# Seven block products of a mixture of experts: y tiles joined on another engine and at another time, and bank-opening products on another operand

## The chip, the cores and the metric

One core of one Trainium2 chip. The metric is the device time of one execution in microseconds; lower is better. The times below are those of single executions, and the profile is that of one further execution.

## The reference

A gated attention gives the input of a mixture of experts with 16 experts in 4 groups. Cut to what is computed:

```python
# attention: B, S, D = 8, 1856, 256; d_qk = 64
scores = (1.0 / S) * np.matmul(z, z.transpose(0, 2, 1))
attn = np.maximum(scores, 0.0) ** 2
x = (u * np.matmul(attn, v)).reshape(B * S, D)          # 14848 rows of 256
# experts: G = Eg = 4, F = 1024
g_logits = x @ w_group
g_idx = np.argmax(g_logits, axis=1)                     # g_w: its softmax weight
e_logits = xg @ w_expert[g]                             # rows xg of group g
e_idx = np.argmax(e_logits, axis=1)                     # e_w: its softmax weight
h = np.maximum(xg[mask_e] @ w1[g, e], 0.0)
ye = h @ w2[g, e]
out[tok_idx] = (g_w * e_w)[:, None] * ye
```

Each row of x goes to one expert; its result is scaled by one number and written to the row that it came from.

## The kernel before, in words

**Stages.** The attention part takes about the first half of the time. It routes its rows as it goes: a row, with its weight and its number, is scattered to a bucket of its expert in DRAM. Then come the experts, sorted by how many rows they hold: the first four (NOLD = 4) in 12 blocks of up to 512 rows, the other 12 (numbers 4 to 15) each as a pair of halves of equal width (512 rows each for expert 4, 424 for expert 14). All matmuls are done in parts: an operand is split into a high and a low part, and a product is low x high, high x high and high x low.

**A block (experts 0 to 3).** `phase1` (L784) is the first product and the relu: 8 slices f of 128 hidden rows with 6 matmuls each, evicted by ACT (L797) and DVE (L803). `phase2_t` (L848) is the second product, transposed: for each of two halves d of the 256 outputs, 24 matmuls (8 slices f, 3 parts q) into one bank. ACT copies the bank out as 16-bit halves (L872, L877); SP then issues one transposing DMA for each tile t of 128 rows (L882), from `yp` to `yr`. What brings a tile to its end is `finish(t, m)` (L886): a **join** of the halves into a tile y (L888, DVE), the **scale** by the row's weight (L894 on DVE for a block, L896 on ACT for a pair), and the **scatter** to the output (L897, issued by POOL). `phase2_t` does not run `finish`; it returns one such function for each tile, and the caller keeps them in the list `unsent` and pops them where it chooses.

**A pair (experts 4 to 15).** The first product of both halves together is done by seven block products in place of eight (`duo_phase1`, L1256): w1 and x are combined beforehand (`split_w1`, L1173, 8 steps; `split_duo`, L1223, 12 steps; both on DVE and ACT), and for each of four g there are products m = 1 to 7 of three matmuls each (L1274). They add up in PSUM banks that are never opened anew: ACT copies product 1 to bank Y (L1288) and product 5 to SBUF (L1291), DVE adds (L1293, L1297), ACT and DVE evict (L1282, L1283). The order of the 28 products is the list `seq` (L1304). In it, product 6 of a g adds onto the copy that L1288 has made. Then `phase2_t` runs for half 0 and for half 1. POOL splits w2 in eight steps (`split_w2`, L1191; L1197 and L1198), into w2 tiles that the second product reads; w2 comes by the tiles r0 and r1, into which the next expert's w1 is loaded when the splits are done.

**Order.** Program order is the order in which a scheduler is told of the instructions; it gives each engine a fixed order of its own, from the dependences and its own estimates. Instructions under `pin` keep their order among each other on their engine; in the pair stage, all of TensorE's instructions keep program order. So the places at which `finish` and the other small steps are called matter for DVE, ACT and POOL. In a pair they are these:
- The loop over `prods` (L1383) interleaves the products with the steps of `split_w2`, with the overflow planner (`planned`, L1386, at every fourth product) and with four pops of `unsent` (L1388, at lengths 12, 9, 6 and 3).
- In half 0, `slots` (L1405) holds the last product and steps of `split_w1` and `split_duo` (`chore`); a slot (d, k) is ahead of matmul k of half d of the outputs.
- In half 1, `slots` holds further such steps, four pops of `unsent` at (0, 3), (0, 9), (0, 15) and (0, 21) (L1433), and from (1, 10) on the first four products of the next expert (`lead`).

So half 0's four tiles are finished in half 1 and half 1's four in the next expert's first product: 92 tiles in all in `phase2_t` of the pairs. The last half (L1442) is done in another way, by `phase2`, which pops what is left in its first tile.

**The planner** (`plan`, L1043) works out an overflow path with some 47 small DVE steps; eleven of them work on 1024 elements. In the blocks it is advanced at L1327, from block 5 on, at every second f.

**Buffers.** Tiles of one tag share a number of buffers; a tile gets one when an earlier tile of that tag has had its last access. `y` has 3, `tm` has 2 (used in the pairs by `phase2` alone), `meta` (weights and row numbers of a half) has 4, and `at` has 3: w1's high part of a block expert, and later the tiles a, s and t of `split_w1` (L1180, L1182, L1188). In the hand-over to the pairs, `duo_banks` (L1248) opens the four banks y0, y1, z0 and z1 with one matmul each (L1254); its operand is `wt["h"][0]`, the high part of w1 of expert 3.

Of the kernel before, what the change touches and what calls it, by code (L numbers as in the profile page):

```python
# [9 lines left out]
F32 = mybir.dt.float32  # L10
F32R = mybir.dt.float32r
BF16 = mybir.dt.bfloat16
I32 = mybir.dt.int32
# [6 lines left out]
P = 128  # L20
# [9 lines left out]
def tile_glu_attn_moe(  # L30
# [715 lines left out]
    NOUT = sum((n + P - 1) // P for n in [bk[2] for bk in blocks] + [n for d in duos.values() for n in d])  # L746
    oviews = dram_disjoint_views(out, NOUT)
    ocnt = [0]
    rows_b = {}
    wts = {}  # L750

# [2 lines left out]
    def load_x(name, r0, n):  # L754

        xp = new_pl(f"xp_{name}").rearrange("p (g q) -> p g q", g=4)
        nc.sync.dma_start_transpose(xp[:, :, 0:n], bucket16[ds(r0, n), 0:2 * D])
        meta = sb("meta", [P, 4, 2], I32, 4, f"meta_{name}")
        nt = (n + P - 1) // P
        nc.sync.dma_start(  # L760
            meta[:, 0:nt, :], bucket[ds(r0, nt * P), D:D + 2].rearrange("(t p) w -> p t w", p=P)
        )
        return xp, meta
# [84 lines left out]
    def phase2_t(name, wt, hs, meta, n, outs, between, po=None, slots=(), order=range(NF)):  # L848
        po = po or [bank(ps_o, "o", f"yT_{name}_{d}") for d in range(ND)]
        order = list(order)  # L850
        yp = sb("ut", [P, ND, 512], F32, 2, f"yp_{name}").rearrange("p c q -> p (c q)").bitcast(U16)
        yr = new_rows(f"yr_{name}")
        tiles = [(t, min(P, n - t * P)) for t in range((n + P - 1) // P)]
        full, part = n // P, n % P

        yg = yp.rearrange("p (t g q) -> p t g q", g=4, q=P)
        if part:
            nc.gpsimd.memset(yg[:, full, :, part:P], 0)
        for d in range(ND):
            between(d)  # L860
            o = po[d][:, 0:n]
            prods = [(f, q) for f in order for q in range(3)]
            if d == 0:
                prods.sort(key=lambda x: x[1] == 2)
            for at, (f, q) in enumerate(prods):
                for fn in slots and slots.pop((d, at), ()):
                    fn()
                w0 = (f % 2) * 512 + (D if q == 0 else 0) + d * P
                nc.tensor.matmul(o, wt["2"][f // 2][:, w0:w0 + P], hs[f][q // 2][:, 0:n],  # L869
                                 start=(at == 0), stop=(at == 3 * NF - 1))  # L870
            if full:
                nc.scalar.copy(  # L872
                    out=yg[:, 0:full, 2 * d:2 * d + 2, :],
                    in_=o[:, 0:full * P].bitcast(U16).rearrange("p (t q h) -> p t h q", q=P, h=2),
                )
            if part:
                nc.scalar.copy(  # L877
                    out=yg[:, full, 2 * d:2 * d + 2, 0:part],
                    in_=o[:, full * P:n].bitcast(U16).rearrange("p (q h) -> p h q", h=2),
                )  # L880
        for t, m in tiles:
            nc.sync.dma_start_transpose(  # L882
                yr[:, t, 0:D].bitcast(U16).rearrange("p (g d) -> p g d", d=P),
                yg[:, t].rearrange("p g q -> p (g q)"),
            )
        def finish(t, m):  # L886
            y = sb("y", [P, D], F32, 3, f"y_{name}_{t}")
            pin(nc.vector.tensor_copy(  # L888
                out=y[0:m].bitcast(U16).rearrange("p (d q h) -> p d h q", d=ND, h=2),
                in_=yr[0:m, t, 0:D].bitcast(U16).rearrange("p (d h q) -> p d h q", d=ND, h=2),  # L890
            ))
            cw = meta[0:m, t, 0:1].bitcast(F32)
            if isinstance(name, int):
                nc.vector.tensor_scalar(out=y[0:m], in0=y[0:m], scalar1=cw, scalar2=None, op0=ALU.mult)  # L894
            else:
                nc.scalar.activation(out=y[0:m], in_=y[0:m], func=AF.Copy, scale=cw)  # L896
            nc.gpsimd.indirect_dma_start(  # L897
                out=outs(),
                out_offset=bass.IndirectOffsetOnAxis(ap=meta[0:m, t, 1:2], axis=0),
                in_=y[0:m],  # L900
                in_offset=None,
                bounds_check=N - 1,
                oob_is_err=False,
            )

        return [lambda t=t, m=m: finish(t, m) for t, m in tiles]
# [295 lines left out]
    def duo_rows(e):  # L1202
        n1, n2 = duos[e]
        r0 = regs(e)[1]
        lst = []
        at = 0
        while at < 2 * n1:
            n = min(512, 2 * n1 - at)
            xp = new_pl(f"xp_w{e}_{at}").rearrange("p (g q) -> p g q", g=4)
            nc.sync.dma_start_transpose(xp[:, :, 0:n], bucket16[ds(r0 + at, n), 0:2 * D])  # L1210
            lst.append((at, n, xp))
            at += n
        metas = []
        for h, n in enumerate((n1, n2)):
            meta = sb("meta", [P, 4, 2], I32, 4, f"meta_w{e}_{h}")
            nt = (n + P - 1) // P
            nc.sync.dma_start(
                meta[:, 0:nt, :], bucket[ds(r0 + h * n1, nt * P), D:D + 2].rearrange("(t p) w -> p t w", p=P)
            )
            metas.append(meta)  # L1220
        duo_x[e] = (lst, metas)
# [23 lines left out]

    banks = {}

    def duo_banks(wt):  # L1248
        for k in ("x0", "w", "p0"):
            banks[k] = bank(ps_s, "s", f"duo_{k}")  # L1250
        banks["p1"] = bank(ps_m, "m", "duo_p1")
        for k in ("y0", "y1", "z0", "z1"):
            banks[k] = bank(ps_o, "o", f"duo_{k}")
            nc.tensor.matmul(banks[k], wt["h"][0][:, 0:P], wt["h"][0][:, 0:512], start=True, stop=True)  # L1254

    def duo_phase1(e):  # L1256
        w = duos[e][0]
# [54 lines left out]
    for i, (e, r0, n) in enumerate(blocks):  # L1312
# [10 lines left out]
        def mid(f):  # L1323
            if i < NEARLY:
                early(i)
            elif i > 2 * NEARLY and f % 2 == 0:
                next(planned, None)  # L1327
            if i + 1 == NB and f > 3 and unsent:
                unsent.pop(0)()
# [42 lines left out]

        unsent = phase2_t(i, wts[e], hs, rows_b.pop(i)[1], n, next_view, mid2) or unsent

    duo_banks(wts[NOLD - 1])
    pe_order = ExitStack()
    pe_order.enter_context(tc.manual_schedule(engines={mybir.EngineType.PE}))
    wt = {"2": [wst[f"w{k}"] for k in range(4)]}
# [1 line left out]
    for e in range(NOLD, NE):  # L1380
        more = e + 1 < NE
        build2 = split_w2()
        while len(prods) > 1:  # L1383
            next(build2, None)
            if len(prods) % 4 == 0:
                next(planned, None)  # L1386
            if unsent and len(prods) < 14 and len(prods) % 3 == 0:
                unsent.pop(0)()  # L1388
            if more and len(prods) == 8:
                duo_w1(e + 1)  # L1390
                duo_rows(e + 1)
# [10 lines left out]
        def chore(n):  # L1402
            return lambda: [next(work, None) for _ in range(n)] if more else None

        slots = {(0, 4): [prods[0]]}  # L1405
        for d in range(ND):
            for k in range(0 if d else 6, 24, 3):
                slots.setdefault((d, k), []).append(chore(1))
# [5 lines left out]
        if more:  # L1414
# [15 lines left out]
            slots[(1, 10)] = slots.get((1, 10), []) + [ahead_products]  # L1430
            for k in (12, 14, 18, 20):
                slots.setdefault((1, k), []).append(lead(k))
            for k in (3, 9, 15, 21):  # L1433
                slots.setdefault((0, k), []).append(lambda: unsent.pop(0)() if unsent else None)
            unsent += phase2_t(f"w{e}_1", wt, hs[1], duo_x[e][1][1], n2, next_view, lambda d: None, po, slots)
            hs, prods = nxt["hs"], nxt["prods"]
        else:
# [75 lines left out]
```

## Time and profile before

| | us |
|---|---|
| median of 3 runs | 1468.46 |
| lowest and highest of them | 1468.35, 1470.37 |
| the profiled execution | 1471.43 |
| its span, first to last instruction | 1469.6 |
| TensorE matmuls busy (share) | 1428.8 (97%) |
| VectorE (DVE) busy | 1231.9 (84%) |
| ScalarE (ACT) busy | 1020.1 (69%) |
| GpSimd (POOL) busy | 394.0 (27%) |

The mean granted clock of TensorE is 0.989 of full speed. How to read the rows: PE is TensorE, SP issues DMAs. Matmuls are pipelined, so that one starts before the one ahead of it has ended; the distance of their starts is what one takes, and their "busy" time is modelled. "idle before <- X" is the time for which an engine did nothing ahead of an instruction, and what ended it. L12 is line 12 of the kernel before. Times are microseconds from the start of the span, if nothing else is said.

### The profile page before, as it was taken

Reading aid. Unit: us, or ns where it says so; the run is one execution under the profiler, and the core shown is the slowest. Engines: PE = TensorE matmul, PEld = TensorE weight load, DVE = VectorE, ACT = ScalarE, POOL = GpSimd, SP = SyncE. Lnnn points to the kernel's source line nnn. Section 1 sums busy time; section 2 is a strip of 40 time slices with the busy share of each in tenths; the row PEclk is TensorE's granted clock in tenths of the full one; section 3 lists DMA queues with packets and bytes.
Section 4 is the critical chain, followed back from the end, with each engine's and each line's share of the span. In section 5 each row is a group of like instructions: output and inputs, shape, how many; then the busy total and the mean of one; then the engine's idle time right before and its main releaser. Section 6 shows DMA issues by size and latency. Waiting matters only on the chain.

```text
span 1469.6 us, 22695 instructions
## 1 busy us (share of the span) xinstructions
PE 1428.8 (97%) x6981; PEld 1229.3 (84%) x6981; DVE 1231.9 (84%) x2460; ACT 1020.1 (69%) x1824; POOL 394.0 (27%) x462
## 2 busy tenths in 40 slices
PE   9999999999999999999999999979999999999986
PEld 7898888888888878888788989957788888888885
DVE  7889999989989899999986585977888888787873
ACT  8887887878877788777774444445666666666653
POOL 0002112220122202222205212333333444443433
PEclk9999999999999999999999999989999999999999
DMA  9998969889799887997884555514454454454531
GB/s 319 327 238 226 242 169 267 206 233 222 181 256 217 221 221 185 254 225 193 202 212 103 149 120 113 122 54 107 128 131 125 121 132 122 121 135 118 133 88 46
DMA packets 400045, 256.48 MB, mean 175 GB/s; under 512 B 244131, under 2 KB 355262, under 8 KB 399920
## 3 DMA queue, kind: packets, MB, share of 16 engines
q1 hardware_dynamic: 387984, 223.97, 61.6%
q0 software_dynamic: 11856, 30.90, 7.1%
q8 instruction: 55, 0.90, 0.3%
q14 instruction: 70, 0.57, 0.1%
q10 hardware_dynamic: 80, 0.13, 0.0%
HBM read 108.29 MB, written 89.21 MB: 134 GB/s over the span
## 4 chain that ended last, share of the span: by engine, by line
PE 78%; DVE 10%; issue 5%; DMA 2%; POOL 2%; ACT 2%; SPq 0%; DVEq 0%; ACTq 0%; POOLq 0%
PE o L403 13%; PE o L404 13%; PE o L406 12%; PE duo_p L869 11%; PE yT L869 5%; PE duo_y L1274 4%; PE sc L366 4%; PE sc L367 4%; PE ph L792 2%; PE duo_x L1274 2%; PE ph L793 2%; PE ph L794 2%; PE duo_w L1274 2%; PE duo_p L1274 1%; PE duo_z L1274 1%
## 5 line engine op out<-in xcount | busy, mean ns | idle before, releaser
L403 PE MATMUL o<-ah,vl 128*128 128x512 f32 (+2 forms) x960 | 354.5, 370 | 0.6 <-DVE ah L378 0.4
L404 PE MATMUL o<-ah,vh 128*128 128x512 f32 (+2 forms) x960 | 354.3, 369 | 0.0
L406 PE MATMUL o<-al,vh 128*128 128x512 f32 (+2 forms) x896 | 329.2, 370 | 0.0
L638 POOL DMA_INDIRECT bucket<-rows,di x121 | 137.9, 1140 | 376.4 <-issue 219.1
L370 ACT ACTIVATE r<-sc 128x512 f32<-128x512 f32 (+2 forms) x312 | 178.2, 571 | 66.5 <-PE sc L367 41.1
L403 PEld LDWEIGHTS o<-ah,vl 128*128 128x128 f32 x960 | 180.2, 188 | 30.5 <-DVE ah L378 0.8
L404 PEld LDWEIGHTS o<-ah,vh 128*128 128x128 f32 x960 | 180.2, 188 | 29.0
L381 DVE TENSOR_TENSOR al<-r,ah 128x512 fp32r<-128x512 f32 (+2 forms) x280 | 187.8, 671 | 17.3 <-PE pk L603 0.5
L406 PEld LDWEIGHTS o<-al,vh 128*128 128x128 f32 x896 | 167.9, 188 | 26.9 <-DVE al L381 0.7
L869 PE MATMUL duo_p<-hh_w,duo_w 128*128 128x496 f32 (+9 forms) x692 | 183.9, 379 | 4.0 <-POOL duo_w L1198 3.6
L377 ACT ACTIVATE r<-r 128x512 f32<-128x512 f32 (+2 forms) x284 | 174.2, 613 | 9.0
L869 PEld LDWEIGHTS duo_p<-hh_w,duo_w 128*128 128x128 f32 x692 | 131.6, 191 | 22.4 <-POOL duo_w L1198 4.2
L378 DVE CAST ah<-r 128x512 fp32r<-128x512 f32 (+2 forms) x284 | 117.4, 413 | 25.1 <-ACT r L377 20.3
L897 POOL DMA_INDIRECT out_dram<-y_w,meta_w x92 | 94.2, 1023 | 141.6 <-ACT y_w L896 123.0
L366 PE MATMUL sc<-zm,z2h 128*128 128x512 f32 (+2 forms) x312 | 120.3, 386 | 0.1
L367 PE MATMUL sc<-zm,z2l 128*128 128x512 f32 (+2 forms) x312 | 118.9, 381 | 0.0
L869 PE MATMUL duo_p<-hl_w,duo_w 128*128 128x496 f32 (+9 forms) x346 | 106.5, 379 | 0.0
L306 DVE STREAM_TRANSPOSE mt<-r 128x512 f32<-128x512 f32 x147 | 103.7, 705 | 0.6
L356 DVE TENSOR_TENSOR al<-at,ah 128x512 fp32r<-128x512 f32 (+1 forms) x168 | 94.9, 578 | 3.3 <-ACT ah L355 2.8
L355 ACT CAST ah<-at 128x512 fp32r<-128x512 f32 (+1 forms) x168 | 86.2, 532 | 9.1 <-DMA at<-sym 3.7
L869 PE MATMUL yT<-hh,w_e 128*128 128x512 f32 (+6 forms) x384 | 82.9, 334 | 0.0
L897 POOL DMA_INDIRECT out_dram<-y,meta x37 | 40.9, 1105 | 130.8 <-DVE y L894 124.9
(238 smaller groups left out, 2869.1 us busy)
## 6 DMA issues: line engine op xcount, KB each, us to landing
sym<-mt SPq DMA_DIRECT2D x126, 256.0 KB
duo_r<-in_w_dram SPq DMA_DIRECT2D x48, 512.0 KB
at<-sym SPq DMA_DIRECT2D x84, 256.0 KB
bucket<-padrow SPq DMA_DIRECT2D x32, 660.0 KB
at<-sym SPq DMA_DIRECT2D x84, 160.0 KB
vr<-in_v_dram SPq DMA_DIRECT2D x23, 512.0 KB
ut<-in_uT_dram SPq DMA_DIRECT2D x23, 512.0 KB
raw_e<-in_w_dram SPq DMA_DIRECT2D x16, 512.0 KB
```

Source lines behind the costliest of these rows:

```text
L366: held(nc.tensor.matmul(ps[:, 0:w], z2h[:, ks], zm, start=True, stop=False))
L367: held(nc.tensor.matmul(ps[:, 0:w], z2l[:, ks], zm, start=False, stop=True))
L370: held(nc.scalar.activation(out=a, in_=ps[:, 0:w], func=AF.Relu, scale=1.0 / S))
L377: held(nc.scalar.activation(out=a, in_=a, func=AF.Square))
L381: held(nc.vector.tensor_sub(out=al, in0=a, in1=f32(ah)))
L403: held(nc.tensor.matmul(o, vl[:, dsl], ah, start=(i == 0), stop=False))
L404: held(nc.tensor.matmul(o, vh[:, dsl], ah, start=False, stop=end and al is None))
L406: held(nc.tensor.matmul(o, vh[:, dsl], al, start=False, stop=end))
L638: nc.gpsimd.indirect_dma_start(out=views[(b * NQ + 2 * half + hs[h]) * NT + i], out_offset=bass.IndirectOffsetOnAxis(ap=di[0:n, i0 + i:i0 ...
L869: nc.tensor.matmul(o, wt["2"][f // 2][:, w0:w0 + P], hs[f][q // 2][:, 0:n], start=(at == 0), stop=(at == 3 * NF - 1))
L897: nc.gpsimd.indirect_dma_start(out=outs(), out_offset=bass.IndirectOffsetOnAxis(ap=meta[0:m, t, 1:2], axis=0), in_=y[0:m], in_offset=None, ...
L1274: nc.tensor.matmul(out, a, b, start=(q == 0 and m in (1, 5)), stop=(q == 2), skip_group_check=True)
```

## The change

The joins of the pairs' tiles go to ACT, except those with t = 3, which stay on DVE with their scale; y tiles of the pairs take their buffer in turn from `y` (three times) and `tm` (twice). `meta` gets 7 buffers. The pops leave the first product of the pairs: six slots in half 0 and three in the second output half of half 1 take their place; with eight tiles for each expert, five are then finished in half 0 (one from half 0 of the expert before, four from its half 1) and three in half 1. The planner leaves the pairs and is advanced at every f of the blocks. The bank-opening products read tile a.

```diff
@@ phase2_t: finish @@
         def finish(t, m):
-            y = sb("y", [P, D], F32, 3, f"y_{name}_{t}")
-            pin(nc.vector.tensor_copy(
+            old = isinstance(name, int)
+            ycnt[0] += 1
+            tag, bufs = ("tm", 2) if not old and ycnt[0] % 5 > 2 else ("y", 3)
+            y = sb(tag, [P, D], F32, bufs, f"y_{name}_{t}")
+            cw = meta[0:m, t, 0:1].bitcast(F32)
+            join = dict(
                 out=y[0:m].bitcast(U16).rearrange("p (d q h) -> p d h q", d=ND, h=2),
                 in_=yr[0:m, t, 0:D].bitcast(U16).rearrange("p (d h q) -> p d h q", d=ND, h=2),
-            ))
-            cw = meta[0:m, t, 0:1].bitcast(F32)
-            if isinstance(name, int):
+            )
+            if old or t == 3:
+                pin(nc.vector.tensor_copy(**join))
                 nc.vector.tensor_scalar(out=y[0:m], in0=y[0:m], scalar1=cw, scalar2=None, op0=ALU.mult)
             else:
+                pin(nc.scalar.copy(**join))
                 nc.scalar.activation(out=y[0:m], in_=y[0:m], func=AF.Copy, scale=cw)
@@ load_x and duo_rows @@
-        meta = sb("meta", [P, 4, 2], I32, 4, f"meta_{name}")
+        meta = sb("meta", [P, 4, 2], I32, 7, f"meta_{name}")
@@ duo_banks @@
-            nc.tensor.matmul(banks[k], wt["h"][0][:, 0:P], wt["h"][0][:, 0:512], start=True, stop=True)
+            nc.tensor.matmul(banks[k], wst["a"][:, 0:P], wst["a"][:, 0:512], start=True, stop=True)
@@ blocks: mid @@
-            elif i > 2 * NEARLY and f % 2 == 0:
+            elif i > 2 * NEARLY:
                 next(planned, None)
@@ pairs @@
         while len(prods) > 1:
             next(build2, None)
-            if len(prods) % 4 == 0:
-                next(planned, None)
-            if unsent and len(prods) < 14 and len(prods) % 3 == 0:
-                unsent.pop(0)()
...
+        def send():
+            if unsent:
+                unsent.pop(0)()
+
         slots = {(0, 4): [prods[0]]}
+        for d, k in ((0, 9), (0, 15), (0, 21), (1, 3), (1, 9), (1, 15)):
+            slots.setdefault((d, k), []).append(send)
...
-            for k in (3, 9, 15, 21):
-                slots.setdefault((0, k), []).append(lambda: unsent.pop(0)() if unsent else None)
+            for k in (0, 4, 8):
+                slots.setdefault((1, k), []).append(send)
```

## Rows read from the trace of the kernel before

**Rows 1.** Busy time in stretches: start:end, length, PE, PEld, DVE, ACT, POOL, clock, DMA.
```profile
900.00:940.00 40.00, 39.97 (x286) 39.28 (x285) 31.18 (x63) 17.60 (x39) 8.79 (x9) 1.00 0.57 113
940.00:980.00 40.00, 30.87 (x118) 23.81 (x117) 27.87 (x42) 14.30 (x21) 18.44 (x14) 0.83 0.42 103
1121.20:1160.62 39.42, 39.42 (x182) 33.72 (x181) 32.95 (x53) 27.11 (x49) 16.43 (x18) 1.00 0.49 130
1359.58:1402.72 43.14, 37.33 (x188) 34.38 (x186) 35.61 (x58) 27.41 (x51) 19.09 (x20) 0.99 0.45 116
```

**Rows 2.** Timeline of PE at full clock: start, length, line, tiles, count.
```profile
986.35 0.85 PE L1274 MATMUL duo_p<-duo_x,duo_p 128*128 128x512 f32 x3
987.04 0.85 PE L1274 MATMUL duo_w<-duo_x,duo_s 128*128 128x512 f32 x3
```

**Rows 3.** Four further stretches, columns as in rows 1; PE's instructions in brackets.
```profile
961.82:979.11 17.29, 8.17 (x18) 5.50 (x19) 14.74 (x17) 4.88 (x7) 12.65 (x9) 0.61 0.24 68
990.00:1000.00 10.00, 8.22 (x29) 6.24 (x29) 10.00 (x19) 6.94 (x12) 1.35 (x2) 0.83 0.08 28
1340.00:1350.00 10.00, 8.20 (x33) 7.20 (x33) 4.91 (x9) 5.31 (x11) 4.53 (x7) 0.83 0.42 109
1396.00:1410.00 14.00, 9.32 (x34) 8.48 (x34) 8.23 (x14) 5.98 (x11) 4.22 (x3) 0.76 0.22 56
```

**Rows 4.** Table of PE's waits, 760 to 1470 us: sum, times, longest.
```profile
PE duo_y L1274 <- ACT duo_y L1288: 8.3, 11, 1.8
```

**Rows 5.** Timeline of PE around the hand-over.
```profile
961.19 0.63 PE L1254 MATMUL duo_z<-w1h_e 128*128 128x512 f32 x2
...
967.74 1.22 PE L1274 MATMUL duo_y<-duo_x,duo_t 128*128 128x512 f32 x2 [5.93 <-ACT duo_x L1241]
```

**Rows 6.** Timeline of ACT there.
```profile
961.90 1.05 ACT L1188 CAST duo_t<-duo_r 128x1024 fp32r<-128x1024 f32 x1
966.65 1.04 ACT L1241 CAST duo_x<-duo_r 128x1024 fp32r<-128x1024 f32 x1 [3.70 <-DVE duo_r L1240]
```

**Rows 7.** Timeline of DVE there: a join, and an operation of the planner.
```profile
963.46 0.46 DVE L888 COPY y<-yr 128x512 uint16<-128x512 uint16 x1 [9.56 <-DMA yr<-yp]
...
967.42 1.23 DVE L1093 TENSOR_TENSOR ov_big<-ov_le,ov_it 128x1024 f32<-128x1024 f32 x1 [0.80 <-POOL duo_w L1197]
```

**Rows 8.** Timelines of POOL and PE near 1400 us.
```profile
1399.17 2.19 POOL L897 DMA_INDIRECT out_dram<-y_w,meta_w  x1 [2.43 <-ACT y_w L896]
...
1402.72 1.78 PE L869 MATMUL duo_p<-hh_w,duo_w 128*128 128x424 f32 x4 [3.65 <-POOL duo_w L1198]
```

**Rows 9.** Timelines of DVE, ACT and PE near 1263 us.
```profile
1262.61 0.46 DVE L888 COPY y_w<-yr_w 80x512 uint16<-80x512 uint16 x1 [2.29 <-DMA out_dram<-y_w,meta_w]
...
1263.15 0.51 ACT L896 ACTIVATE y_w<-y_w,meta_w 80x256 f32<-80x256 f32 x1 [1.96 <-DVE y_w L888]
...
1265.02 0.89 PE L1274 MATMUL duo_y<-duo_x,duo_t 128*128 128x456 f32 x3 [1.73 <-ACT duo_y L1288]
```

**Rows 10.** Groups by line from 900 us on (busy us, mean ns), and one ACT copy.
```profile
L888 DVE COPY y_w<-yr_w 128x512 uint16<-128x512 uint16 x92 | 51.5, 570 | 26.5 <-DMA yr_w<-yp_w 17.1 <-DMA out_dram<-y_w,meta_w 5.0 <-issue 3.3
...
L896 ACT ACTIVATE y_w<-y_w,meta_w 128x256 f32<-128x256 f32 x92 | 45.8, 509 | 24.4 <-DVE y_w L888 17.3 <-issue 6.4 <-ACT h_w L1282 0.2
...
910.30 0.59 ACT L872 COPY yp<-yT 128x512 uint16<-128x512 uint16 x1 [2.54 <-PE yT L869]
```

**Rows 11.** Timelines of SP, POOL and DVE: transposes issued, what waits for them, last scatter.
```profile
1249.76 5.76 SPq L882 DMA_TRANSPOSE yr_w<-yp_w  x4
1256.80 0.28 POOL L858 MEMSET yp_w<- 128x224 uint16 x1 [14.48 <-DMA yr_w<-yp_w]
...
1450.60 5.73 SPq L882 DMA_TRANSPOSE yr_w<-yp_w  x4
1453.06 0.46 DVE L888 COPY y_w<-yr_w 128x512 uint16<-128x512 uint16 x1 [9.89 <-DMA yr_w<-yp_w]
1463.33 0.97 POOL L839 DMA_INDIRECT out_dram<-y_w,meta_w  x1 [0.30 <-issue]
```

More of the change, by code (lines that the diff above doesn't have):

```diff
@@ L748, in tile_glu_attn_moe @@
     ocnt = [0]
+    ycnt = [0]
     rows_b = {}
@@ L1214, in duo_rows @@
         for h, n in enumerate((n1, n2)):
-            meta = sb("meta", [P, 4, 2], I32, 4, f"meta_w{e}_{h}")
+            meta = sb("meta", [P, 4, 2], I32, 7, f"meta_w{e}_{h}")
             nt = (n + P - 1) // P
@@ L1246, in tile_glu_attn_moe, with duo_banks @@
     banks = {}
-    def duo_banks(wt):
+    def duo_banks():
         for k in ("x0", "w", "p0"):
@@ L1373, in tile_glu_attn_moe @@
         unsent = phase2_t(i, wts[e], hs, rows_b.pop(i)[1], n, next_view, mid2) or unsent
-    duo_banks(wts[NOLD - 1])
+    duo_banks()
     pe_order = ExitStack()
```

## The prediction

> **What bounds the kernel now.** I read the stretches first, since the change lies behind the attention part. In the last single-block stage TensorE is busy 39.97 of 40 us, and in a wide expert of the seven-product stage 39.42 of 39.42: nothing can be gained there. It is 30.87 of 40 where the one stage hands over to the other, and 37.33 of 43.14 in expert 13 [rows 1]. So the question is what ends the gaps of TensorE, and how long each lasts with the clock that follows it.
>
> To price a gap with its clock I count matmuls. At full clock three matmuls of 512 columns follow each other in 0.69 us, so one takes 0.23 us [rows 2]; by its columns one of 440 takes 0.20 and one of 424 0.19 (estimates by the ratio of widths). [...]
> Together 27.4 us. The table of waits adds 8.3 us in 11 waits for ACT's copy at L1288 [rows 4]; 1.8 of it lies in the third stretch, which leaves 6.5. **The pool of what can be won is 33.9 us.**
>
> **The hand-over.** TensorE's last work before its gap is the pair of bank-opening products on w1h_e, ending at 961.82; it resumes at 967.74 and names ACT's cast at L1241 [rows 5]. ACT did L1188 (the cast into tile t) at 961.90, right behind that end, and L1241 only at 966.65, after 3.70 us of waiting for L1240 on DVE [rows 6]. The code joins the two: "at" has three buffers, a and s hold two, and t needs the third, w1h of the last single-block expert. It is free when its last reader is done, and that reader is the opening product. L1239 writes over the tile that L1188 reads, so x5 hangs on it. A join waiting 9.56 us for its transpose and the planner's 1.23 us operation stood in the same DVE queue [rows 7].
>
> **The change, part by part.**
> 1. Opening products read tile a. They issue the same four matmuls. The third "at" buffer is then free after the last block's first product, one second product (48 x 0.23 = 11.0 us) earlier, and L1188, L1239, L1240, L1241 move up into time in which DVE stood idle for 9.56 us [rows 7]. I take the whole 13.2 us, between 9 (some of the last operands still late) and 13.2.
> 2. No joins and no planner in the first product's time. In the stretch from 990 DVE was busy 10.00 of 10 [rows 3]; the block's four joins and the planner's steps leave it. I take the 3.3 us. In expert 13 the wait of 3.65 us is for POOL's split of w2, and POOL had stood 2.43 us behind a y tile before issuing its scatter, which took 2.19 [rows 8]. No scatter stands between those splits any more: I take 7.5. What is late next is the w1 load that waits for the splits; it comes earlier too.
> 3. Three y buffers become five. The wait at 1262 shows what three cost: the fourth join waited 2.29 us on DVE for a scatter to free its buffer, ACT's scale waited 1.96 behind it, L1288 came late, and TensorE lost 1.73 [rows 9]. Of the eight joins of an expert, five now come in the first half of the second product and three in its second half, at least four matmuls apart. This pattern is behind the third stretch (3.4) and, with the joins' load, the other 6.5. I take 9.9, between 5 and 9.9.
> 4. Joins on ACT. Of 92, those with t = 3 stay on DVE (23), 69 move. DVE loses 69 x 0.570 = 39 us over the stage. An ACT copy of the same 512 halves took 0.59 (the source was PSUM), so ACT gains 41 us, less 23 scales of 0.51 that go to DVE [rows 10]. ACT had 12.3 of 39.4 us free per expert, DVE 6.5 [rows 1], so the sum fits: 6 x 0.59 less 2 x 0.51 is 2.5 us more on ACT. The place is the difficulty: three joins stand before L1288 in the second half, where ACT formerly had only their scales. At most that makes L1288 3 x 0.59 = 1.8 us later in each of 11 experts, 20 us; at least nothing. As ACT has room, and four scales leave its first product, I take 0.5 us, 5.5 in all.
> [...]
> 5. The join waits on ACT. Behind the waiting copy stand the evictions and L1288. The four transposes of a half were issued from 1249.76 and had all landed by 1256.80, when a memset that needs their source began; the first of a set took from 1450.60 to 1453.06, 2.46 us [rows 11]. In between, the third lands about 5.5 us after the first issue (estimate); its join stands 24 + 8 matmuls of 0.21 us, 6.7 us, after the end of the half. So it has landed, with about 1 us in hand: cost nothing, up to the wait of the second rival.
> 6. The planner's steps go to every f of the blocks. Nineteen of its 47 steps move from the seven-product stage to blocks up to the eleventh; four are like the row's 1.23 us [rows 7], the rest small (taken at 0.2 each), some 8 us of DVE in a stage where DVE was busy 31.18 of 40 and TensorE never waited [rows 1]. I take 0.5 us, from 0 to 3.
> 7. Metadata buffers, seven for four: they only let tiles live longer; the loads are the same. Zero, covered by the earlier issue.
> 8. The end. The last four joins are popped at the same place, the last scatters follow each other on POOL, and the last is issued at 1463.33 [rows 11]. ACT's 0.59 for DVE's 0.46: zero, within 1 us.
>
> **The sum.** 13.2 + 3.3 + 7.5 + 9.9 - 5.5 - 0.5 = 27.9 us. The profiled execution took 1471.43 us (span 1469.6), 3 us above the median of the three runs, 1468.46. Its 1471.4 becomes 1443.5; against the median that is 1468.5 - 28 = **1440.5**.
>
> **The rivals.**
> *The wait only changes engines* (0.17). ACT is the one that evicts; joins and scales in its queue could hold L1288 and the banks as the joins on DVE do now. For it: the 1.96 us of ACT's wait in rows 9 is of this kind. Against it: two more buffers and later slots. Then parts 2 and 3 give only the 3.3 us of the stretch at 990, and the hand-over its 13.2: with the 5.5 and 0.5 off, 10.5, and 1458.
> *Slower: ACT waits for the transposes* (0.06). The place is the second half, joins one to three. If SP issues the transposes after its gather for the next expert, the rows land later than the slots and L1288 stands behind the join. A wait of 1.8 us cost 3.4 with its clock [rows 3, 4]; eleven of them cost 37.4, against 33.9 - 0.5 won: 1472.5. It decides from about 3 us of loss per expert.
> [...]
> *The opening product does not hold the buffer* (0.07). L1188 stands right behind L1291 in ACT's order, and might be there for another reason. Then the 13.2 stay: 14.7 won, 1454.
> *Nothing in sum* (0.04): gains and new waits cancel, 1468.
>
> **How the numbers follow.** My forecast has 0.66. Its low end is all 33.9 us with no new wait, 1434.5, and 3 us for gaps outside the four stretches: 1431. To leave out no more than 2 in 10 the range has to take in the first and third rival: up to 1460, 2 us past the first. A measurement of this kernel tells about 0.2%, 3 us, from no change; faster by more than that are the forecast and the first and third rival, 0.66 + 0.17 + 0.07, less 0.01 for a first rival that turns out worse: 0.89; the same 0.05; slower 0.06.
>
> **What would show it.** In the changed profile L1188 should stand some 12 us before the opening products end, TensorE should have no gap there and a granted clock of 1.00; DVE should be less busy in the first product and ACT by 2 to 3 us more per expert; the wait for POOL's splits of w2 in expert 13 should be gone. Waits of TensorE for L1288 with ACT waiting for a transpose would be the second rival; L1188 still behind L1291 the third. I am wrong in the main if the seven-product stage is shortened by less than 15 us, or if waits appear in the block stage with a planner's step before them.

## The result and the profile after

The changed kernel takes 1451.69 us (median of 4 runs, 1446.83 to 1454.91) against 1469.4 in the same session: a ratio of 0.9877 [0.9847, 0.9906], 17.7 us or 1.2% faster. The forecast was 28 us. The profiled execution is its slowest run, 1454.91 us with a span of 1453.1.

Three times of TensorE's timeline split the 16.5 us by which the span is shorter: the start of the second pair of bank-opening products (961.19 before, 958.18 after), that of the first piece of the first wide expert's second product (992.60, 975.88), and TensorE's end (1458.12, 1440.02). So 3.0 us come from ahead of the hand-over (1.7 of it from attention, which the change does not touch), 13.7 from the hand-over and the first product, and 1.4 from all the rest of the seven-product stage, where the forecast had expected most of the other half. The tail gives 1.6 back (11.5 us from TensorE's end to the last instruction, now 13.1). These splits are of one profiled execution each.

Busy time in stretches of the changed kernel, columns as in [rows 1]:

```profile
920.00:960.00 40.00, 40.00 (x232) 35.44 (x231) 31.14 (x52) 20.68 (x35) 14.52 (x12) 1.00 0.50 115
958.00:976.00 18.00, 18.00 (x80) 14.73 (x79) 13.47 (x21) 12.15 (x21) 4.50 (x5) 1.00 0.33 88
1066.00:1085.00 19.00, 17.62 (x80) 14.67 (x79) 13.50 (x20) 12.97 (x21) 14.39 (x7) 1.00 0.63 153
1396.00:1410.00 14.00, 11.50 (x48) 9.47 (x47) 7.43 (x12) 9.57 (x19) 12.10 (x12) 0.88 0.28 78
```

The hand-over has no gap and the full clock, where [rows 3] had 0.61. The third stretch has two of the long scatters described below. The last stretch does not hold the work of the one at 1396 in [rows 3], since the changed kernel is ahead by then; it shows a new wait, of 2.03 us for L1242 at 1400.92. The matmuls of the old stretch, with the wait for GpSimd's split of w2 among them, stand at 1381.49 now and take 6.37 us where they took 14.28.

ACT's timeline shows why the hand-over has no gap. The cast into tile t (L1194, formerly L1188) stands at 945.67 instead of 961.90 [rows 6], and L1247 (formerly L1241) at 952.90, before the opening products:

```profile
945.67 1.04 ACT L1194 CAST duo_t<-duo_r 128x1024 fp32r<-128x1024 f32 x1
...
952.90 1.05 ACT L1247 CAST duo_x<-duo_r 128x1024 fp32r<-128x1024 f32 x1 [4.21 <-DVE duo_r L1246]
```

The table of waits of the changed kernel, PE's first, then two of ACT's (L1294 is the former L1288):

```profile
PE duo_y L1280 <- ACT duo_y L1294: 9.7, 6, 4.1
PE duo_w L1280 <- ACT duo_x L1242: 2.0, 1, 2.0
PE duo_y L1280 <- DVE duo_x L1177: 1.8, 4, 0.5
...
ACT y_w L901 <- DMA out_dram<-y_w,meta_w: 11.7, 6, 3.7
...
ACT y_w L901 <- DMA yr_w<-yp_w: 4.6, 3, 2.3
```

Against [rows 4] there are fewer waits for ScalarE's copy (6 for 11), but they are longer, up to 4.1 us for 1.8, and in sum dearer (9.7 for 8.3). ACT's join L901 waits for transposes little; it waits for **scatters**, which give y buffers back. The groups by line say what became of these (scatters, the joins and scales of ACT, the joins of DVE):

```profile
L903 POOL DMA_INDIRECT out_dram<-y_w,meta_w x92 | 162.5, 1766 | 155.1 <-DVE y_w L899 84.9 <-ACT y_w L902 52.6 <-issue 10.8
...
L901 ACT COPY y_w<-yr_w 128x512 uint16<-128x512 uint16 x69 | 52.8, 775 | 16.4 <-DMA out_dram<-y_w,meta_w 11.7 <-DMA yr_w<-yp_w 4.6
L902 ACT ACTIVATE y_w<-y_w,meta_w 128x256 f32<-128x256 f32 x69 | 34.5, 513 | 0.4
...
L898 DVE COPY y_w<-yr_w 112x512 uint16<-112x512 uint16 (+9 forms) x23 | 10.4, 453 | 14.9 <-ACT y_w L902 14.9
```

A scatter held GpSimd for 1023 ns on average before (its group by line: 94.2 us for the same 92); now it is 1766. Before, none took over 2.19 us in this stage; now eleven take more than 3, the longest 8.09. All start inside a second product, between its 26th and its 65th of 96 matmuls, where VectorE splits the next expert's operands. Two of them, around 1200 us, in timelines of POOL, DVE, ACT and PE (SBUF is the memory in which the tiles lie, PSUM that of the banks):

```profile
1193.81 5.22 POOL L903 DMA_INDIRECT out_dram<-y_w,meta_w  x1 [11.27 <-DVE y_w L899]
1199.34 5.24 POOL L903 DMA_INDIRECT out_dram<-y_w,meta_w  x1 [0.30 <-issue]
1204.88 0.97 POOL L903 DMA_INDIRECT out_dram<-y_w,meta_w  x1 [0.30 <-ACT y_w L902]
...
1197.12 1.79 DVE L1233 COPY duo_r<-xp_w 128x832 uint16<-128x832 uint16 x3
1198.80 0.63 DVE L1177 TENSOR_TENSOR duo_x<-duo_r,duo_x 128x464 fp32r<-128x464 f32 x1
1199.34 0.64 DVE L1240 TENSOR_TENSOR duo_r<-duo_r 128x464 f32<-128x464 f32 x1
...
1203.07 0.63 DVE L1246 TENSOR_TENSOR duo_r<-duo_r,duo_r 128x464 f32<-128x464 f32 x1
1210.03 1.12 DVE L1177 TENSOR_TENSOR duo_x<-duo_r,duo_x 128x928 fp32r<-128x928 f32 x1 [6.33 <-ACT duo_x L1247]
...
1208.41 0.76 ACT L901 COPY y_w<-yr_w 128x512 uint16<-128x512 uint16 x1 [3.73 <-DMA out_dram<-y_w,meta_w]
1209.05 0.95 ACT L1247 CAST duo_x<-duo_r 128x928 fp32r<-128x928 f32 x1
...
1210.93 0.57 ACT L1294 COPY duo_y<-duo_x 128x464 f32<-128x464 f32 x1
...
1211.55 1.46 PE L1280 MATMUL duo_y<-duo_x,duo_t 128*128 128x464 f32 x3 [4.07 <-ACT duo_y L1294]
```

Read it from the second line. DVE runs subtractions from SBUF to SBUF without a pause from 1198.80 until 1203.70. The scatter issued at 1199.34 ends at 1204.58, 0.88 us behind DVE's last one, which is about what a scatter takes alone (0.97 us for the next one, at 1204.88, with DVE idle), and its data land at 1208.39. The next join on ACT needs its buffer and stands 3.73 us; behind it in ACT's queue are L1247, for which DVE waits 6.33, and L1294, for which TensorE waits 4.07. The same chain stands at 1087 (TensorE 3.65). That is the hypothesis that the runs test: **the new slots put scatters beside VectorE's splits, the scatters are drawn out, and what they hold is the y buffers**.

### The profile page after: what moved, and what is told of

It reads as the page before. It is cut to its first block, busy times and chain, and to the rows that moved or that the text cites. A ratio compares the mean times of both kernels' runs of the same rounds, so it can differ in the third digit from the quotient of the medians.

```text
span 1453.1 us, 22618 instructions
## 1 busy us (share of the span) xinstructions
PE 1421.8 (98%) x6981; PEld 1226.9 (84%) x6981; DVE 1206.7 (83%) x2414; ACT 1060.6 (73%) x1870; POOL 460.9 (32%) x462
## 4 chain that ended last, share of the span: by engine, by line
PE 81%; issue 6%; DMA 4%; ACT 3%; DVE 2%; POOL 1%; SPq 0%; POOLq 0%; ACTq 0%; DVEq 0%
PE o L403 14%; PE o L404 14%; PE o L406 13%; PE yT L870 7%; PE duo_p L870 6%; PE sc L366 5%; PE sc L367 5%; PE duo_y L1280 5%; DMA out_dram<-y_w,meta_w 3%; PE ph L793 2%; PE ph L794 2%; PE ph L795 2%; PE duo_p L1280 2%; PE duo_x L1280 1%; ACT y_w L901 1%
## 5 line engine op out<-in xcount | busy, mean ns | idle before, releaser
L903 POOL DMA_INDIRECT out_dram<-y_w,meta_w x92 | 162.5, 1766 | 155.1 <-DVE y_w L899 84.9
L903 POOL DMA_INDIRECT out_dram<-y,meta x37 | 44.3, 1198 | 137.1 <-DVE y L899 130.0
```

What stands on the lines that cost most here:

```text
L903: nc.gpsimd.indirect_dma_start(out=outs(), out_offset=bass.IndirectOffsetOnAxis(ap=meta[0:m, t, 1:2], axis=0), in_=y[0:m], in_offset=None, ...
```

## The experiments

Each kernel was timed in rounds beside the kernel before on the same chip. Chips differ (before took 1468 to 1473), so I compare ratios; a difference of 0.01 is 14.7 us.

| run | what | median us | ratio to before [95%] |
|---|---|---|---|
| changed kernel | | 1451.7 | 0.9877 [0.9847, 0.9906] |
| e1 | before + new opening operand | 1466.0 | 0.9950 [0.9931, 0.9968] |
| e2 | changed, old opening operand | 1461.0 | 0.9927 [0.9906, 0.9949] |
| e3 | changed, seven y buffers | 1443.0 | 0.9790 [0.9769, 0.9811] |
| e4 | changed, old places of the sends | 1460.2 | 0.9914 [0.9897, 0.9931] |
| e5 | changed, joins on VectorE | 1466.1 | 0.9993 [0.9978, 1.0008] |
| e8 | e3, old places of the sends | 1459.7 | 0.9908 [0.9887, 0.9930] |
| e9 | changed, VectorE reads PSUM in between | 1487.0 | 1.0134 [1.0117, 1.0150] |
| e10 | before + seven y buffers | 1457.0 | 0.9927 [0.9910, 0.9943] |
| e11 | e3, joins on VectorE | 1450.5 | 0.9887 [0.9869, 0.9904] |
| e12 | changed, three y buffers | 1481.7 | 1.0059 [1.0041, 1.0078] |
| e13 | changed, planner back | 1461.2 | 0.9924 [0.9907, 0.9941] |
| e14 | e3, all joins on ScalarE | 1436.6 | 0.9760 [0.9738, 0.9782] |

**The hand-over: e1, e2 and e13.** e1 makes the new opening alone, e2 takes it out of the changed kernel:

```
-            nc.tensor.matmul(banks[k], wt["h"][0][:, 0:P], wt["h"][0][:, 0:512], start=True, stop=True)
+            nc.tensor.matmul(banks[k], wst["a"][:, 0:P], wst["a"][:, 0:512], start=True, stop=True)
```

> The kernel before, with the four bank-opening products reading tile a and nothing else changed. If the third buffer of at was held by the opening products (my theory), TensorE has no gap between the last block and the first pair, and nearly the whole gain of the change comes from here: 13 to 17 us, so 1452 to 1457 against 1469. If the gain of the change comes from the joins and the five buffers, this one stays within 4 us of the kernel before.

> The changed kernel, with the opening products on w1h of the last single-block expert again. Theory: the gap of TensorE at the hand-over is back and the kernel loses 11 to 15 us against the changed one, so 1463 to 1467, as the rest of the change nets about nothing. Rival (the rest of the change is worth 10 us or more by itself): 1452 to 1459.

e13 puts the planner's steps back to every second f of the blocks, and into the first product:

```
-            elif i > 2 * NEARLY:
+            elif i > 2 * NEARLY and f % 2 == 0:
...
+            if len(prods) % 4 == 0:
+                next(planned, None)
```

> The changed kernel with the planner's steps where they were: every second f of the blocks, and four times in each first product. My forecast took 0.5 us against the move. Theory: VectorE is the engine with the least slack in the pair stage (48.5 us more on it made the kernel 36 us slower), so some 8 us of small steps back in that stage cost 3 to 7 us; rival (they fit in idle time): within 2 us of the changed kernel, about 1.2% faster than before.

Measured: e1 gains 0.5%, 7 us, half of what I expected; e2 loses 0.5% (7 us) against the changed kernel, less than the 11 to 15 (their intervals just meet); e13 loses 0.47%, 6.9 us, at the top of its range. The length from the second opening pair to the first piece of the second product, from each profile, shows where:

| kernel | from opening pair to second product, us | from there to TensorE's end, us |
|---|---|---|
| before | 31.4 | 465.5 |
| e1 (opening alone) | 23.6 | 471.9 |
| e2 (everything else) | 24.8 | 455.8 |
| e13 (all but the planner) | 22.3 | 461.8 |
| e4 (old sends) | 17.7 | 467.2 |
| changed kernel | 17.7 | 464.1 |
| e3, e14 | 17.7, 17.7 | 450.7, 443.5 |
| e12 (three buffers) | 17.7 | 488.6 |

The gap had two causes in a row. The opening operand alone takes off 7.8 us: L1188 stands at 948.04 in e1, and in e2 its successor is back at 961.10, right behind the opening products. Then other waits appear, as TensorE's timeline of e1 shows (the last one already in the second product):

```profile
960.07 0.63 PE L1254 MATMUL duo_z<-duo_a 128*128 128x512 f32 x2
...
969.48 1.65 PE L1274 MATMUL duo_x<-duo_x,duo_p 128*128 128x512 f32 x3 [2.57 <-DVE hl_w L1283]
...
987.82 0.96 PE L1274 MATMUL duo_y<-duo_x,duo_a 128*128 128x512 f32 x3 [3.06 <-DVE duo_p L1297]
```

DVE is late there. e13, with the opening new and the sends moved, has 22.3: so of the 5.9 us between e1 and the changed kernel 4.6 are the planner's; its steps of 1.2 us each stand in DVE's queue. e4, with the old sends, has 17.7: the joins cost nothing in this first product. The second column is from one profile each, and executions of the changed kernel differ by 8 us: small differences in it mean nothing (e2's profiled execution is its fastest, the changed kernel's its slowest; the changed kernel's has two of the long waits for L1294, e2's has one).

**The buffers: e3, e10 and e12.** e3 adds two y buffers, halves of a tile that is idle in this stage; e10 does the same to the kernel before; e12 gives the changed kernel its three back.

```
-            tag, bufs = ("tm", 2) if not old and ycnt[0] % 5 > 2 else ("y", 3)
-            y = sb(tag, [P, D], F32, bufs, f"y_{name}_{t}")
+            turn = ycnt[0] % 7
+            if not old and turn > 4:
...
+                y = lgy[0][:, (turn - 5) * D:(turn - 4) * D]
+            else:
+                tag, bufs = ("tm", 2) if not old and turn > 2 else ("y", 3)
+                y = sb(tag, [P, D], F32, bufs, f"y_{name}_{t}")
```

> The changed kernel with seven y buffers in the pair stage (two halves of a tile that is idle there). Theory: scatters on GpSimd are drawn out to 5 us while VectorE works on SBUF without a pause, they hold the y buffers, and the join on ScalarE waits for one; with two more buffers the joins' waits for the scatters (11.7 us in 6) fall below 3 us and TensorE's waits for the copy L1294 (9.7 us in 6) below 5; 4 to 8 us faster than the changed kernel, 1444 to 1448, though the scatters stay as long. Rival (the joins' own work on ScalarE holds up the evictions): no difference within 2 us, and the waits for L1294 stay at 8 us or more.

> The kernel before with seven y buffers in the pair stage and nothing else changed. Theory: the waits of VectorE's join for a scatter (5.0 us in 4) vanish, and with them those of ScalarE's scale behind it; TensorE's waits for L1288 (8.3 us in 11) fall to some 5, as the others of them come from joins in the first product; the gap at the hand-over stays: 3 to 8 us faster than before. Rival (buffers were no limit before the change): within 2 us.

> The changed kernel with three y buffers as before; opening, joins on ScalarE and slots stay. It prices the two added buffers. My forecast took 9.9 us for them. Theory now (the drawn-out scatters make each buffer worth more than that at the new slots; two beyond five were worth 12 us): 12 to 20 us slower than the changed kernel, so within 5 us of the kernel before. Rival (the first two buffers are the easy part, the change's gain is in the joins): 4 us or less slower than the changed kernel.

Measured: e3 is 0.87% faster than the changed kernel, 12.8 us, more than my 4 to 8; e10 10.7 us faster than before (3 to 8 expected); e12 26.8 us slower than the changed kernel and 0.6% slower than before. All three theories have the right sign and are too small. In e3 the scatters are as long as ever (ten over 3 us, up to 8.07; mean 1760 ns), but nobody waits for them: no wait of ACT for out_dram of the y_w tiles is left among its longer ones, and TensorE's waits are

```profile
PE duo_y L1287 <- DVE duo_x L1184: 1.3, 3, 0.5
PE duo_y L1287 <- ACT duo_y L1301: 1.3, 2, 1.1
PE duo_y L1287 <- DVE duo_p L1310: 1.1, 1, 1.1
```

9.7 us for L1294 (here L1301) have become 1.3. The gain stands where the long waits stood: from one second product to the next, the experts of the waits of 3.65 and 4.07 us took 45.5 and 44.1 us in the changed kernel and take 40.5 and 38.2 in e3, 10.9 of the 13.4 us by which the second column above differs. In e12 it is the other way round, in the group of ACT's joins:

```profile
L901 ACT COPY y_w<-yr_w 128x512 uint16<-128x512 uint16 x69 | 53.2, 772 | 49.5 <-DMA out_dram<-y_w,meta_w 30.6 <-issue 16.2 <-DMA yr_w<-yp_w 2.8
```

So the buffers are the resource, and with three of them the new slots and joins are worse than the old arrangement.

**What draws the scatters out: e9.** Seven reads of an idle PSUM bank per expert are put among VectorE's splits; the values go to a spare tile and are not used.

```
+        def window():
+            if more:
+                w = duos[e][0]
+                pin(nc.vector.tensor_copy(out=sb("zm", [P, 512], F32, 2, f"win_w{e}")[:, 0:w], in_=banks["w"][:, 0:w]))
...
+                if k % 2:
+                    slots[d, k].append(window)
```

> The changed kernel with seven more VectorE operations per expert among the splits of the first half, each reading an idle PSUM bank (128 x 512) into a spare tile that nothing reads; 77 operations of about 0.65 us, 50 us of VectorE in all. Theory (a scatter gets on only while VectorE isn't working from SBUF to SBUF): each read of PSUM is a window for GpSimd; the scatters of 5 us fall below 3 and their mean from 1.77 to 1.4 us or less, and TensorE's waits for L1294 shrink, the time is 0 to 6 us better although VectorE has more to do. Rival (the scatters are slow because of the DMA traffic of that half, loads of w1 and rows): they stay at 5 us and more, and the added work makes the kernel slower.

Measured: the scatters go part of the way that the theory says, and the time does not. Timelines of POOL and DVE in e9, at the same expert as the 5.33 us scatter at 1069.23 of the changed kernel:

```profile
1074.08 2.01 POOL L903 DMA_INDIRECT out_dram<-y_w,meta_w  x1 [16.19 <-ACT y_w L902]
1076.40 1.73 POOL L903 DMA_INDIRECT out_dram<-y_w,meta_w  x1 [0.30 <-ACT yp_w L878]
...
1073.49 1.25 DVE L1414 COPY win_w<-duo_w 128x496 f32<-128x496 f32 x2
...
1077.90 0.65 DVE L1414 COPY win_w<-duo_w 128x496 f32<-128x496 f32 x1
```

The mean falls to 1488 ns (1.4 us or less was expected), those over 3 us from eleven to six (longest 4.68; none was expected), ACT's waits for scatters from 11.7 us to 3.7. The loads of w1 and of rows are the same, which speaks against DMA traffic as the cause. But the kernel is 2.6% slower than the changed one, 38 us for 48.5 us of added work:

```profile
PE duo_y L1280 <- ACT duo_x L1247: 12.8, 6, 5.7
PE duo_y L1280 <- DVE duo_p L1303: 11.4, 7, 2.6
PE duo_w L1280 <- DVE duo_x L1177: 2.9, 5, 1.1
```

VectorE finishes the splits late, and with them L1247, which needs L1246's result. That was the part I had not seen: time added on VectorE among the splits cost about 0.8 of its length.

**The engine of the joins: e5, e11 and e14.** In e5 all joins are on VectorE and all scales on ScalarE, as before the change; e11 is the same with seven buffers; e14 moves the joins of t = 3 to ScalarE as well, with their scales, on seven buffers.

```
-            if old or t == 3:
-                pin(nc.vector.tensor_copy(**join))
+            pin(nc.vector.tensor_copy(**join))
+            if old:
...
-                pin(nc.scalar.copy(**join))
```

and e14:

```
-            if old or t == 3:
+            if old:
```

> The changed kernel with all joins on VectorE and all scales on ScalarE, as before the change; slots, five buffers and the opening stay. Theory (buffers held by drawn-out scatters are what costs, whichever engine joins): VectorE waits for a scatter to give a buffer back, and while it waits it leaves GpSimd free, so its waits are shorter than ScalarE's (11.7 us in 6); ScalarE loses 53 us of joins; within 4 us of the changed kernel on either side, 1450 to 1460 on this chip. Rival (the move to ScalarE is a gain by itself, as VectorE is the fuller engine): 6 us or more slower than the changed kernel, 1460 to 1468.

> The changed kernel with seven y buffers and with all joins on VectorE (scales on ScalarE): the engine of the joins alone against the run with seven buffers and joins on ScalarE (29.9 us faster than before). Theory: once no join waits for a buffer, ScalarE does the joins in time that it has, and VectorE, the fuller engine, is 31 us fuller with them; 2 to 8 us slower than with joins on ScalarE, 1445 to 1451 on a chip where before takes 1473. Rival (the engine doesn't matter): within 2 us of it.

> Seven y buffers, and all joins on ScalarE, those of t = 3 too, with their scales: VectorE loses 23 joins of 0.45 and 23 scales of 0.35 us, 18 us in all, ScalarE gains 29. Rival A (VectorE is still the tightest engine): 3 to 8 us faster than with seven buffers and t = 3 on VectorE (2.1% faster than before). Theory: that kernel has hardly a gap of TensorE left in the pair stage, and ScalarE, with more than 90% to do, comes late with evictions: 0 to 5 us slower than it.

Measured: e5 is no faster than the kernel before, 17 us slower than the changed kernel; e11 14 us slower than e3; e14 about 4 us faster than e3, though their intervals overlap. My theory for e5 falls, and for e11 was too small; the move to ScalarE is itself a gain. e5 shows how the two causes feed each other, in timelines of POOL and DVE:

```profile
1189.23 10.92 POOL L902 DMA_INDIRECT out_dram<-y_w,meta_w  x1 [12.95 <-ACT y_w L901]
1200.45 1.00 POOL L902 DMA_INDIRECT out_dram<-y_w,meta_w  x1 [0.30 <-ACT yp_w L878]
...
1198.70 0.62 DVE L1245 TENSOR_TENSOR duo_r<-duo_r,duo_r 128x464 f32<-128x464 f32 x1
1201.89 0.46 DVE L897 COPY y_w<-yr_w 128x512 uint16<-128x512 uint16 x1 [2.57 <-DMA out_dram<-y_w,meta_w]
```

With the joins on it, VectorE's run is longer, the scatter lasts until that run ends (10.92 us), and then the next join on VectorE waits for the buffer: 29.0 us in 15 such waits, where the changed kernel has 11.7 on ScalarE. The first item of TensorE's waits in e5 is then

```profile
PE duo_w L1279 <- DVE duo_x L1176: 12.1, 4, 4.4
```

In e14 only four scatters take over 3 us, and TensorE's waits in the stage come to 2.7 us:

```profile
PE duo_y L1287 <- DVE duo_p L1310: 1.1, 1, 1.1
PE duo_y L1287 <- ACT duo_y L1301: 0.9, 1, 0.9
PE duo_y L1287 <- issue: 0.5, 1, 0.5
PE duo_p L871 <- DVE hl_w L1296: 0.2, 1, 0.2
```

I had expected ScalarE to come late, taking it for more than 90% busy; it was busy 335.8 of 450 us in this stage of e3 (980 to 1430), and 356.7 of 444 in e14 (980 to 1424), so it has the room. This is the best version found, 2.4% faster than before: two more buffers and an `if` against the changed kernel.

**The places of the sends: e4 and e8.** The sends are popped again in the first product and in the first output half of half 1, with five buffers (e4) and seven (e8).

```
+            if unsent and len(prods) < 14 and len(prods) % 3 == 0:
+                unsent.pop(0)()
...
-        for d, k in ((0, 9), (0, 15), (0, 21), (1, 3), (1, 9), (1, 15)):
-            slots.setdefault((d, k), []).append(send)
...
-            for k in (0, 4, 8):
-                slots.setdefault((1, k), []).append(send)
+            for k in (3, 9, 15, 21):
+                slots.setdefault((0, k), []).append(send)
```

> The changed kernel, but the y tiles are sent again in the first product's time and in the second half's first product, as before the change; joins stay on ScalarE, five buffers. Theory: in the first product VectorE reads PSUM and the scatters take about 1.0 us each (mean 1.77 in the changed kernel), so the joins don't wait for them: 1446 to 1451, as far as the joins among the evictions let it. Rival (ScalarE's joins in front of the evictions are what costs): TensorE waits more for ScalarE's evictions in the first product, 1455 to 1461.

> Seven y buffers, joins on ScalarE as changed, but the y tiles sent at the places of the kernel before. With five buffers this order of sends was 5 us slower than the new one. Theory (in the first product joins and scales stand among the evictions on ScalarE, which no buffer mends): 4 to 9 us slower than the new slots with seven buffers, so 1.5 to 1.8% faster than before. Rival (the slots matter through the buffers alone, and the old ones have the shorter scatters): as fast as the new slots or faster, 2.1% or more.

Measured: e4 is 5.4 us slower than the changed kernel by the ratios, against my theory, though their intervals overlap; its scatters are shorter as the theory said (mean 1233 ns). e8 is 17 us slower than e3, more than the 4 to 9 expected: at the old places two more buffers bring nothing (0.9908 and 0.9914). In the first product the joins stand among the evictions, as TensorE's waits in e8 say:

```profile
PE duo_y L1287 <- ACT duo_y L1301: 7.2, 15, 0.9
PE duo_y L1287 <- DVE duo_p L1310: 5.4, 4, 2.3
PE duo_p L871 <- DVE hl_w L1296: 2.9, 3, 1.3
```

Many short waits, none for a buffer. So the new slots are right where there are buffers enough for the scatters that they draw out.

## Why the prediction was right, and where its sum was wrong

The direction, the range and the main mechanism of the hand-over held: L1188's successor moved 16 us up, the gap and its slow clock (0.61 in [rows 3], now 1.00) are gone, and no wait took its place. The forecast's 28 us were 10 too many. That the range held is in part luck: it had been stretched to 1460 to take in two rivals, and 1451.7 lies nearer to their 1458 and 1454 than to 1440.5. By my own sign of being wrong in the main, less than 15 us off the seven-product stage, it was close: 15.1 us from the second opening pair to TensorE's end.

TensorE does its matmuls of that stage in the same order in both kernels, so the two profiles can be laid side by side. Over the matmuls of the four priced stretches the changed kernel is shorter by 13.3, 2.3, 3.6 and 7.9 us, 27.2 in all, where the forecast had 27.4: the lengths of the four in [rows 3] less their matmuls at full clock, 17.29 - 18 x 0.23 = 13.2, 10 - 29 x 0.23 = 3.3, 10 - 33 x 0.20 = 3.4 and 14 - 34 x 0.19 = 7.5 us. What failed is the rest. It was to win 6.5 us and pay 6.0, and it lost 12.1; 10.4 of these stand in two experts, which took 40.0 and 39.2 us from one second product to the next and now take 45.5 and 44.1, those of the waits of 3.65 and 4.07 us. The prices of the parts below are those of undoing each alone. In the order of the forecast:

1. *Opening operand, 13.2 us.* Mechanism right, and the whole change won the 13.2; but of these 7 us are the operand's, by e1 and e2. I gave the whole stretch to the tile, although [rows 7] had a planner's operation in the same queue; e13 shows that 4.6 us of what followed were the planner's.
2. *No joins and no planner in the first product, 3.3 and 7.5.* The wait for GpSimd's split is gone, as said (it stood in expert 14, whose 424 columns [rows 8] show, not in 13), and the stretch at 1396 gave 7.9 us; the one at 990 gave 2.3. Later in the same expert a wait for L1242 came in (2.0 us). The place of the sends is worth 5.4 us by e4 (with the overlap said above), and 17 once buffers suffice (e8 against e3).
3. *Three buffers to five, 9.9.* At the new slots it is 26.8 (e12). The step that failed is one that the text left out: it counted joins per half and took it that a scatter gives its buffer back at the new slots as soon as at the old ones (2.19 and 0.97 us in [rows 8, 11]). The new slots lie beside VectorE's splits, where it takes up to 8 us; that cost stands in no part of my sum.
4. *Joins on ScalarE, 5.5 against.* The sign is wrong: 17 us for it (e5), 14 with seven buffers (e11), and some 4 more for the last 23 (e14). I priced a join on ScalarE and let the same join's absence from VectorE count for nothing in this stage. Its own size was off too: 0.775 us, not 0.59. VectorE is the faster at this copy (0.453 us for t = 3); moving it still paid, since VectorE's time was the scarcer: among the splits each us more on it cost 0.8 us (e9).
5. *The waits for transposes, nothing.* Nearly so: ScalarE waited 4.6 us in three.
6. *The planner, 0.5 against.* In the block stage, where I had put this cost, TensorE was busy 180.00 of 180 us (760 to 940). What its leaving the pairs is worth, 6.9 us by e13, is more than the 3.3 that part 2 had for the planner and the joins together.
7. *Metadata buffers* were not tried alone. 8. *The end, zero within 1.* It cost 1.6 us.

Parts 4 and 6 were undervalued for one reason: I valued VectorE by its mean idle time (6.5 of 39.4 us per expert) and not by the waits that end on it. e9 has its price.

The rivals: "the wait only changes engines" is what became of a good part of the seven-product stage: 7.7 of the 9.7 us of waits for L1294 are two waits before which ScalarE stands in a join. Its time, 1458, was 6 us too late, where the forecast was 11 too early, and it named no scatter. That the opening product does not hold the buffer is refuted by e1 and e2, by where the cast into t stands in them. The slower case, waits for transposes on ScalarE, did not come, though its chain (a join standing in front of L1294) did, with another releaser and in 2 experts at full size instead of 11.

The single prices don't add: undoing each part costs 7, 5, 17, 27 and 7 us, 63 in all, and the whole is 18. Each was taken with the others in place, and the buffers pay mainly for what the new slots cost: two of them are worth 26.8 us there (e12), four 10.7 at the old places (e10). The slots alone, on the kernel before, were not run.

## What to carry to other kernels

Before a DMA that GpSimd issues is moved, look at what VectorE does at the new place: beside long runs from SBUF to SBUF, price it by the length of the run and not by its usual microsecond (here 3.99 to 8.09 us in eleven cases, for a mean of 1.02 before), and give its source enough buffers for that. Value an engine's time by whether its queue ends the waits of the bounding engine, not by its mean idle share; here an engine that was busy 344.8 of 464 us in the stage (976 to 1440 in the changed kernel) cost 0.8 us for each us put among its splits. When several changes share a resource, undo them one at a time from the changed kernel: what is measured so is what each protects, not what each adds.

## What the runs showed of the hardware that I had not expected

In these runs a scatter issued by GpSimd was held while VectorE worked from SBUF to SBUF, and the length of VectorE's run without a pause set how long. The one at 1199.34 ended 0.88 us behind the last subtraction at 1203.70 in the changed kernel, and the one of 10.92 us at 1200.15 in e5, 0.83 us behind VectorE's last at 1199.32. A very short pause was mostly enough: of the eleven scatters over 3 us in the changed kernel, nine ended 0.83 to 0.89 us behind the start of a pause in VectorE's row, four of these behind one of about 0.03 us, after which VectorE went on subtracting. One of the four, in timelines of POOL and DVE, with the pause between 1248.08 and 1248.11:

```profile
1243.30 5.63 POOL L903 DMA_INDIRECT out_dram<-y_w,meta_w  x1 [0.30 <-ACT duo_x L1239]
...
1247.46 0.62 DVE L1245 TENSOR_TENSOR duo_r<-duo_r,duo_r 128x456 f32<-128x456 f32 x1
1248.11 0.63 DVE L1246 TENSOR_TENSOR duo_r<-duo_r,duo_r 128x456 f32<-128x456 f32 x1
1248.75 1.11 DVE L1177 TENSOR_TENSOR duo_x<-duo_r,duo_x 128x912 fp32r<-128x912 f32 x1
```

The other two, at 1069.23 and 1193.81, met such a pause too, 2.4 and 2.2 us before their end, but copies followed it; they ended 0.12 us behind the last of these (1198.91 for the second), while a subtraction was already running. That would fit a scatter of two steps, the first held by subtractions and copies and the second by copies alone; it was not tried. Beside evictions that read PSUM a scatter took about as long as alone (0.97 us): in the kernel before, 17 of the pairs' scatters stood where VectorE was busy for more than 95% of their time, and for more than 90% with such operations, and took 0.93 to 1.03 us. One read of PSUM among subtractions was not always enough: the scatter of 4.68 us in e9, at 1252.09, outlasted one of 0.64 us.

What of a scatter is held was not tried. The one at 1199.34, which takes its row numbers from SBUF, took 5.24 us, the first 4.36 of them beside nothing but subtractions of two SBUF tiles; whether it is the reading of these numbers that is held, no run shows.
